# Retention and two MLPs on one core: the hand-kept order table of all 2,323 operations is replaced by another one

## The chip, the cores and the metric

One Trainium2 chip, one core of it. The metric is the device time of one execution in microseconds (us). The kernel before has a median of 588.84 us over three runs (587.54 to 589.17).

## The reference

The input is a retention layer (2 batches, 8 heads, 768 positions, head size 64), and its output x, 1,536 tokens by 512, goes through two MLPs of hidden size 2,048. The first has a rational activation, the second x times sigmoid(x).

```python
for t in range(S):
    state = gamma[None, :, None, None] * state + np.einsum('bhd,bhe->bhde', k[:, :, t], v[:, :, t])
    y[:, :, t] = scale * np.einsum('bhd,bhde->bhe', q[:, :, t], state)
...
h = x @ w_in
P = a[0] + a[1] * h + a[2] * h * h + a[3] * h * h * h
Q = 1.0 + np.abs(b[0]) * np.abs(h) + np.abs(b[1]) * h * h
x = (P / (Q + 1e-06)) @ w_out
...
h = x @ w2_in
return (h * (1.0 / (1.0 + np.exp(-h)))) @ w2_out
```

## The kernel before, in words

**Tiling.** Retention runs as 12 chunks of 128 tokens ("at0" to "at11", `attention`, L426). The MLPs work on three groups of 512 tokens. Every factor of an MLP matmul is split into a high and a low part (`xh`/`xl`, `ih`/`il`, `oh`/`ol`, `gh`/`gl`), and three products of parts stand for one product. The first MLP has 48 steps, s0 to s47 (`step`, L541), each 128 hidden units of one token group. A step is 12 matmuls into a PSUM bank h (L552; banks h0 and h1 in turn up to s19, from s20 on h0, h1, a0 and a1 in turn), a chain on ScalarE and VectorE (L564 to L574), the split of its result into `gh` (ScalarE, L583) and `gl` (GpSimd up to s48, L584), and four projections of three matmuls into the banks acc0 to acc3 (`project`, L605). The second MLP follows in the same manner, partly by sums and differences of blocks (`joint`, L705).

**The chain of a step.** The first five operations read the bank h: ScalarE takes w = |b1 h| (L564) and s1 (L565), VectorE u2 = (w + b0) h (L566), s1 times h (L568) and the next term of the polynomial (L569). Only L566 needs L564, and only L568 and L569 need L565; otherwise the order of the five is free. Then ScalarE takes u2's absolute value, the reciprocal square root and its square (L567, L570, L571), and VectorE ends with three operations (L572 to L574). Up to s16 and from s20 on these put the reciprocal into the bank h itself, so that the bank comes free for the step that is next on it (s+2, from s20 on s+4) at the end of L574.

**Weights.** Each unit u of weights, a pair of steps wide, is loaded (`weights`, L369), rounded and put together by two ScalarE passes (L397, L399) and one VectorE pass (L400, `wt<-wt,raw` in the profile), split by ScalarE (L411) and GpSimd (L416), and some units are spilled to DRAM and read back for later groups (L383, L403).

**Order.** `Flow.op` (L107) records each operation with its engine and with what it must follow by its buffers. Nothing is issued at that point. `Flow.order` (L124) decodes the table `ORDER` (L31) into a permutation of the record, asserts that each operation stands behind those it must follow, and the operations are issued in that order. Each engine runs its own instructions first in, first out, and SyncE issues all DMAs in that order. So the table sets the queue of each engine, and where two engines use one PSUM bank, who goes first. `Op.bank` marks the bank of each ScalarE or VectorE operation that uses one (L117).

```python
places = np.frombuffer(zlib.decompress(base64.b85decode("".join(ORDER))), np.uint16)
done = [self.ops[n] for n in places]
assert all(o.place < f.place for o in done for f in o.feeds)
```

Of the kernel before, what the change touches and what calls it, by code (L numbers as in the profile page):

```python
# [28 lines left out]


ORDER = (  # L31
    'c-jru^TQBk7l7e&p2IiW%eJ{{wY+TGwpOi{wq-Bdwr$%sx7@b)egDG!({;y#G>{e$VgNuahzl{nAPxkG3<B}Nfgm*`f;^BAGC*QT4-EMs0elDfAP',
# [4 lines left out]
    'hV^kMj0eG5m=zf-U;(U&!*MPo$Lcr&M#CTQJr+j7k)W6jCqr!<1u3u@j)Cl01dCz|Oo>0>PuLu%KwX>wQ(+>E#s=6Bd*Gii9g1N~?1_!AHRi;s*b',
    '7_XH0X_eF*p8>v!D+ChPki}w#DLD0>|LbI0tgzA2=50K}no}lW+#ihH*F&XF@yN3GJ~1E`$mABX-0^uo(JaKkSdAa3Yq%`Pc;O;VkTg18^p;fnRV',
    'S4#Fj{0B7SOoPv|_Ph5x_aRK~_opBS+hqbT_mf&LCf}62XSc-FTJuJhe&={BFYS@ZR!ZzHFD{v(?#csF(R^blZiH*ZbXc2Z{)6gpHfYrDg_uv}ri',
    'rsM)%)?>W1&82ZJdGo;T{w$(aXGXMdvOI!#qoFsr{Q+k2y5{IUc_^F4>!R++<>jaP<(*vaXQ||M|d7D;bq*9o8by}30H9)Gz;r+dgu_^hlkiLbPb',  # L40
    '1a4mJ;4;4wbIr+5ty<8|yF-r~%#6;9xc&@nv2=lC9X!%@6}@9+S=z**rhTpa$z5BMK$0}21&NBo3;<7b>5j^IhWiMQ|-?tw38p-uRTyC8lzh>^k_',
    ')ZpPIMh@R_FC4>&5G6znZ*Xo%5Tb>IAyJ4PmWJC1p>0?aILr$%Ld=jjBnjVz`C%U<4avf5>=a^!9-(Jg7LMbBkUV4vnL@^pB4iCIL#mKDbPoF=OU',
    'M?ohe(h*<On&#<q!geg&|J38ghj~;Y#>E<PLGeoKPeb4jA%;q9I;b9)1YLLh<lpxEZd65}{-$6)J>Ep<+lMDu;9-Zzvc};mWWo#14x>ny@<b3b(_',
    'pP&E_?)xw&PHdG1KLyb@~)C#4;A?O|YhT36m=o9jXexZN3AASyX!hrBgC=>3472&5aF#H|{g<nIy@JFZ{u7~nrT^JcggwbJe7!}5babZj-8`g)|G',
    '(J2G8^Xr0DGUh{!i}&cJP41%!LT_T4h_Qaa4g&nTf_12IFt($L%mQxYzxD}p>QNT4GAeO#i65NQaAwj!sM_$#G^E{Bb*2?LwtH3o`uBpI_wO)LIQ',
    'db64A+!gpdxxchoSv`hU2j^jp{+-h{VdPdF8r{tQ#Y=^!*TObO|T=v|l=-iHt2OgJ0<37P0X*c<)|nQ0U&89fP35%h037qU_o`a6u~|H8-cDWs*s',
    'l%29s5&9e=QDjO+mqJn67cPW9I6YO8<dlL&a1P2z59kM~Ma3uzeGSFwN6JOHX@4j|7egK@NqH$M)uuLdJ^+0SKT|&X66#VkdP;36C8eU_T!%_g1}',
    'aVYsXjHJ81$CfQ7p<xWhgoop!SrSI?`|4iDFV&Do6FGA$6edsX8^HpQtl+p~lpe`cpS*LItTQjpTkbfPSH7)SO1qXsSrRb9Wj@m8cL^q0PL72hp!',
    'ImIl)hszEhr4E;^zsRwQ2@ic+P@@!g5bEql}rE%1nc5*cu!+W?gRiK_Uj9O6(+D|R15A~wHw4Eo?Tv|YrXdMlwg*1;Q({J=U^`?<DpVreNT1?}36',
    'K$X=^e1hkUA%-2&{R4^(`Ykop@X!Pj?gmtgD%omI!fDUJMHC5w47GZc)m=B=@=cSE3|{I(LXeUM$mLxMYCun&7__5FP)%|bds*qDSFJiXdiFo|L7',  # L50
    '`JksEZAPSY9MO{-}SMQ~zXL$~NNeWBYFnIrKh`btmu8%5!09G&k_5(ZAncj+EI<sJMN$CpI%jL*?o%EC`*FYTl6I4URO7#x$6GjiY*9E)RfR!+&p',
    'sW=X&X67`Uo$u2HdPwJ~DE~!oC@w$eZ2SW!khGkWUs5iP#|b3|7vprCoAdB1dPc>$1iz!_^dpz#Qk<9baejV5uc-<P8!J0E;}^V}({pLA%GLNiJ)',
    '#2KoU3ygF3UAJJ}2NroRBkf56-{^xdqqYTHKOra~*EQ<+wGs;kNt}Kc>1|kIQpA?#YRz7Z>3|oQX5?1pb~2bAA3m-$_krAg{PR_vH@Un>+H)+<^O',
    'VBbmraq#^g?zqu1H<jTCCD{)1xz>T>nH{nLynfvo39>9O{WS+{ua6@^`wWPKrl_|W47jt77$aQ2IPv<2(gAec^e#5`=OJ2syc_vqu<g%0x@+_XsE',
    'BFW><wIOmR&rBW#of6pcjJrvmb>r}9?FAxHLu}0e2EY9F}}>lc`c`qb$o(P@+qz-)#Vyr;p_a4-}6=e!2j}pJfDZL$UIIZb9o~#;PrfiPxC)~lW*',
    '~DzQZ*nrPP;Za)y&hHK{92q`AzMC9;9f@+QtB7x*L36BU=G(o#P0XO55-Vse+~ODp-pUpbOQmIZQ;zi}E#Ez6{hv=xwZe4ZcheQqtAWTC8<w31$;',
    'NK{EDc_o8HljyQs@<|NIF9qcx2YJMQ3JMF!7}+A5C8K1Ln6gqbOCeb+1>}1vEQ@4~oR(O!SXRka$s$FhsGOClaz=iTVlq~;N;Zinv1O;kl{j)vvP',
    '*GUCpTq<Y?B9aN!Ckl$tk&{yp)n0QdWMHTXI{r%QU$o<7B*SkPC88F3S~}AopdXT$Kt^S}IBzDJMV4bSWXb<dHm->rzr?$PT$Etmoy6T$8(UNG8i',
    '9nIeZpRrH2Tlvy%cX3BH<CP!qqm_C+0a#X&`F#+8x5&A?TYbHgFr7z^E1dXCmHIhCP(rCJ0_Q@PMA@Ah49FT*OQZs87&8j&yx@OZKG=|33IGSDK>',
    'R<9+K1go;M{;RQZ72Uq9{pQV=}YM>rzD}Cl-Ke`UddbeDF4Z4$)Wi)z82Hsnn)9C7x_`+X#sVuqxm&~7Se*6MC)l?Evb36m42_OHI25`HriM}Nol',  # L60
    'RD?WMk^)$g>emeC?wR-0-Qt)k_$p%&FfT39=311+J=^e0WB$uy}Z*NmD$TWBZktfO_fw$xJEMXTyq9izYNZ(2>$Yb8ymJ+!BG)ArgyyXycQD&w@e',
    '{-Mpat4`95+D>O^Fa1Ra>SP_M6LgAB)KU7Uc95yMLr3T)-K@Q}tMt(=T0tvnd9A56w3gP^6*^xB=`8Ig)3l=;)2%vFr|YjeOnS&{?I|mDmoCtqx=',
    '?rPBHgBY^@JYR#oAxC>puNi`)PmetHX4#4%H#LOqc6fU8>h~iJsI|IzU$IFLF-jY9Hw?YqYPN*Lk`}=jeVNuP^kJKG*lUR@dtWy`ZP{fF9KAdQs2',
    'lA96_l(i=KlM#v!fTR-R#{Z0PUt9nUO+7%7<T5oDE`B?_aQN5+VOD7@gCvUX3jFeyHi9Xebx=wHFBTZ$a<c_i()`XV8p6O#9EiYB<l_s*pmewxoK',
    'YC9i%<ZivwZZaEli3jYtar7fm9ixEoh7&X+ReJ!1D$QDEsdqH()O>anWeKbmfpJCN9|#~ZI1n9ne3B((YaRMzUnvaWB=bRi)0xrvPHE@7S}RbG|O',
    'V~EV@Op_!h&mS!T;_Wi6lOus9aWs#s3TYL%^=Rki$9(283HTWAGro>jA$me;CVA**QLTYdY{8dweMX}zqb^|Ra-+iKf#D{OTvm*ufyR>TI_5-VYS',
    'ZILy%hE~g3*a~Z8Ev=I+wbeG?I$K@)!4_D5`^A2?mA1;(*dS|WgY8$VXUlA;HMW6P)SB9QyJTJLstvJWw%FEMD;sC6?VgRdHg?&5w?C|{MfDqY+a',
    '}lpTW9y}ipB7aHrzT`6WeAtZG(-lYc|71+HW?|9@!n+WRESOC-O=5(C*rGn`yHwwwLhD*3PzAdwXVMY_x5)j<&<T^O(NJp4epDZd2^3CH1|w(~j7',
    '4i{sO5ti7<Qw#)WeG(T$l?JtY&vHX~o^u)f~l6W#dZs+Z#jj~tvx1F%J_S#bTbo<jvdpW;lmHnMvu#@(WeX}?AubndRxSrgr_(hB76&(G&9k4@|(',
    '#v=xukQa@MUU^1y{gynkM_ZWNAc5k*bZ8HPvzA-fv0xzvzEp`*%?dg>^1!-&+28pl-Kffp25Yld2K&u8NIG&_UvBA>v;~(<azz8)%OP8$n$v?Z|I',  # L70
    'G^yf^VL_SxLk&6{~n&+QRj%nNuyZ|W_)xOec5-qH*CK>ywcc_q*9+x=HR?VbD&ALoPpNB`6JdMj`4t-Z5%@xq?Rb9qs3<L&$hFXCN&h<Ed$-rn1K',
# [889 lines left out]
```

## Time and profile before

| | before |
|---|---|
| median of three runs | 588.84 us |
| profiled execution | 586.15 us |
| its span, first to last instruction | 584.3 us |
| TensorE (PE) busy | 568.2 us, 97% |
| VectorE (DVE) busy | 436.2 us, 75% |
| ScalarE (ACT) busy | 405.4 us, 69% |
| GpSimd (POOL) busy | 179.9 us, 31% |

The span runs from the first to the last instruction; 1.85 us of the execution lie around it. PE is TensorE's matmuls, and the end of a matmul is modelled. In the waits, "PE h L552 <- DVE s L345" means that TensorE stood still before a matmul of L552 into h, until a VectorE instruction of L345 that wrote s had ended. L330, L338 and L345 are lines of the helpers `act`, `tt` and `stt`, through which most ScalarE and VectorE operations go; the names of their buffers tell them apart.

### The profile page before, as it was taken

The page shows a single profiled execution, that of the slowest core. Times are in us where ns is not written, and L with a number is a line of the kernel's source. Part 1 is how long each engine was busy: PE and PEld are TensorE (multiplying, and loading weights), DVE is VectorE, ACT ScalarE, POOL GpSimd, SP SyncE. Part 2 cuts the span into 40 slices and gives each one's busy share as a digit, 9 for nine tenths or more (in the row PEclk, how much of TensorE's full clock was granted, in tenths as well). Part 3 has the DMA queues.
Part 4 walks back from the last instruction along what each step waited for, and adds up shares of the span by engine and source line. Part 5 has one row for each costly group of instructions (what it writes and reads, how often), then busy time and mean ns, then how long its engine had stood idle before and what let it go on. Part 6 is the DMA issues. An engine that isn't in the chain of part 4 may idle for free.

```text
span 584.3 us, 8254 instructions
## 1 busy us (share of the span) xinstructions
PE 568.2 (97%) x2908; PEld 464.4 (79%) x2908; DVE 436.2 (75%) x679; ACT 405.4 (69%) x697; POOL 179.9 (31%) x143
## 2 busy tenths in 40 slices
...
GB/s 272 344 359 250 260 282 174 140 61 85 108 73 87 130 72 17 2 91 85 7 180 146 215 204 247 270 224 173 115 102 126 134 83 91 54 37 209 294 38 73
DMA packets 42161, 86.36 MB, mean 148 GB/s; under 512 B 4230, under 2 KB 4358, under 8 KB 42120
## 3 DMA queue, kind: packets, MB, share of 16 engines
...
q8 instruction: 23, 0.38, 0.2%
q14 instruction: 18, 0.15, 0.1%
...
## 4 chain that ended last, share of the span: by engine, by line
PE 77%; ACT 10%; DVE 9%; DMA 2%; issue 1%; SPq 0%; ACTq 0%; DVEq 0%
PE acc L605 38%; PE h L552 12%; PE a L552 9%; PE h L768 7%; PE a L768 7%; ACT h L330 2%; DVE s L345 2%; DVE u L345 2%; ACT s L330 1%; DVE wt L345 1%; DMA vn<-in_v_dram 1%; DVE s L338 1%; ACT w L330 1%; ACT raw L330 1%; DVE h L345 1%
## 5 line engine op out<-in xcount | busy, mean ns | idle before, releaser
L338 POOL TENSOR_TENSOR gl<-s,gh 128x512 fp32r<-128x512 f32 x48 | 63.7, 1330 | 117.2 <-ACT gh L330 68.3
L605 PE MATMUL acc<-gh,oh 128*128 128x512 f32 x192 | 75.7, 394 | 0.0
L605 PE MATMUL acc<-gl,oh 128*128 128x512 f32 x192 | 75.0, 391 | 0.2 <-POOL gl L338 0.2
L605 PE MATMUL acc<-gh,ol 128*128 128x512 f32 x192 | 74.8, 390 | 0.0
L605 PE MATMUL acc<-oh,gl 128*128 128x512 f32 x192 | 74.7, 389 | 0.0
L605 PE MATMUL acc<-oh,gh 128*128 128x512 f32 x192 | 74.7, 389 | 0.0
L605 PE MATMUL acc<-ol,gh 128*128 128x512 f32 x192 | 74.7, 389 | 0.0
L552 PE MATMUL h<-xh,ih 128*128 128x512 f32 x168 | 67.1, 400 | 5.5 <-DVE s L345 5.3
L552 PE MATMUL h<-xl,ih 128*128 128x512 f32 x168 | 65.6, 390 | 0.0
L552 PE MATMUL h<-xh,il 128*128 128x512 f32 x168 | 65.5, 390 | 0.0
L345 DVE SCALAR_TENSOR_TENSOR wt<-wt,raw 128x512 int32<-128x512 int32 x64 | 51.1, 809 | 18.8 <-ACT raw L330 13.1
L416 POOL TENSOR_TENSOR il<-wt,ih 128x512 fp32r<-128x512 f32 x36 | 47.7, 1331 | 38.1 <-ACT ih L411 36.1
L416 POOL TENSOR_TENSOR ol<-wt,oh 128x512 fp32r<-128x512 f32 x36 | 48.8, 1362 | 25.1 <-ACT oh L411 20.5
L330 ACT ACTIVATE raw<-raw,par 128x512 int32<-128x512 uint32 x64 | 48.4, 759 | 2.6 <-DMA raw<-in_moe_w_in_dram 2.4
L345 DVE SCALAR_TENSOR_TENSOR s<-s,par,h 128x512 f32<-128x512 f32 x65 | 48.2, 745 | 1.5
L552 PEld LDWEIGHTS h<-xh,ih 128*128 128x128 f32 x168 | 31.5, 188 | 16.2 <-DVE s L345 8.7
L330 ACT ACTIVATE wt<-raw 128x512 f32<-128x512 f32 x64 | 42.1, 661 | 3.0 <-DMA raw<-in_moe_w_out_dram 1.1
L330 ACT ACTIVATE gh<-s 128x512 fp32r<-128x512 f32 x56 | 35.1, 628 | 12.3 <-DVE s L345 5.2
L605 PEld LDWEIGHTS acc<-gl,oh 128*128 128x128 f32 x192 | 36.0, 188 | 8.5 <-POOL gl L338 1.0
L605 PEld LDWEIGHTS acc<-gh,oh 128*128 128x128 f32 x192 | 36.0, 188 | 8.1 <-DVE raw L338 0.3
L605 PEld LDWEIGHTS acc<-oh,gl 128*128 128x128 f32 x192 | 36.0, 188 | 7.6
L605 PEld LDWEIGHTS acc<-oh,gh 128*128 128x128 f32 x192 | 36.0, 188 | 7.5
...
## 6 DMA issues: line engine op xcount, KB each, us to landing
...
```

The costliest lines, as they stand in the source:

```text
L330: lambda: nc.scalar.activation(out=out_, in_=in_, func=func, **kw),
L338: op(eng, dur, rank, lambda: e.tensor_tensor(out=out_, in0=in0, in1=in1, op=alu), reads, writes, port)
L345: lambda: nc.vector.scalar_tensor_tensor(out=out_, in0=in0, scalar=scalar, in1=in1, op0=op0, op1=op1),
L416: e.tensor_tensor(out=sl.t[nm + "l"][:, us], in0=wt.t, in1=sl.t[nm + "h"][:, us].bitcast(F32), op=ALU.subtract)
L552: nc.tensor.matmul(h.t, sl.t[w][:, ws], x[g].t[:, c, :], start=(n == 0), stop=(n == 3 * KD - 1))
L605: nc.tensor.matmul(a.t, a1, a2, start=(first and n == 0), stop=(last and n == 2))
L768: nc.tensor.matmul(b_.t, w[0](c, wlo), x[0](c, xlo), start=(start and n == 0), stop=(n == 5), skip_group_check=True)
```

## The change

The table `ORDER` gets another content: the operations, their buffers, their dependencies and the code that issues them stay as they were. The search that made the new table kept the accesses of ScalarE and VectorE to each PSUM bank in program order, that is, in the order of issue. The strings can't be read by eye; decoded with the three lines above, the two tables compare so:

| queue | operations | at another place | largest move, places | first and last place that differ |
|---|---|---|---|---|
| TensorE | 541 | 154 | 12 | 4, 198 |
| ScalarE | 695 | 300 | 57 | 3, 341 |
| VectorE | 679 | 265 | 133 | 1, 314 |
| GpSimd | 139 | 55 | 13 | 7, 90 |
| SyncE (DMAs) | 268 | 99 | 16 | 0, 125 |

The last TensorE place that differs is the matmul group at 251.2 us of the profile. What the prediction speaks of, decoded:

- Start: SyncE's first loads were qT (at0), qT (at1), vn (at1), two rows of constants, kT (at0), cst; they are qT (at1), vn (at1), a row, vn (at2), cst, a row, qT (at0), kT (at0). On VectorE, the scaling of vn (at1), which needs cst, moves from place 7 to place 1, ahead of the memset of `ones` (place 2) and of `causal` (place 3).
- Ahead of s13's matmuls TensorE no longer has two projections (s9 m2, s10 m3); ahead of the end of s11's chain VectorE no longer has one masking of at11.
- Ahead of s16's matmuls one projection fewer stands (s13 m3 and s12 m0 leave, s12 m1 comes); ahead of the end of s14's chain VectorE no longer has the build of `ident` (L835), but the weight pass of unit 9's second half.
- Ahead of s18's matmuls one projection more stands (s14 m1); ahead of the end of s16's chain `ident` leaves, and a weight pass of unit 10 comes.
- Ahead of s24's matmuls one projection fewer stands; ahead of the end of s20's chain `ident`, one operation of s22 and two of s21 leave.
- Ahead of s32's matmuls nothing changes; ahead of the end of s28's chain two operations of s30 leave. Ahead of s36's matmuls nothing changes; ahead of the end of s32's chain three operations come (the sum of a part out of acc0, and one operation each of s33 and s34).
- Turns: in a step's first five operations the bank passes from ScalarE to VectorE once, or three times (ScalarE, VectorE, ScalarE, VectorE). Three times in the old table: s1, 6, 7, 9, 11, 14, 16, 17, 19, 21, 22, 24, 27, 30, 32, 34, 35. In the new one: s1, 5, 8, 12, 20, 21, 23 to 30, 32, 34, 35. In all others of s0 to s37 it passes once.

```diff
--- before.py
+++ after.py
@@ -29,49 +29,49 @@
 
 
 ORDER = (
-    'c-jru^TQBk7l7e&p2IiW%eJ{{wY+TGwpOi{wq-Bdwr$%sx7@b)egDG!({;y#G>{e$VgNuahzl{nAPxkG3<B}Nfgm*`f;^BAGC*QT4-EMs0elDfAP',
-    'HoIq>vnPLllS#xgaw{gXj<ewV(tPfMie&(m^Ij38|nA6ojl$2!4bV@I7RK!%!CTLJl|r3b7$4l!Kq32$Y1XkPWiKDX0zA;V9IE!cZFOKruK2$Dla',
...
+    'c-jru1H%yJ769Pm_k7u2w#`+m<z?HpwQ9ArEqmFvZQHiF<+jCp|Hbp9fwX`S1M&btdWZ=C@gRUhT!;*bAQt2Ufy9sjQbQ8R2(dvSJ}^XqgpdI8Lm',
+    'bErNg*oag5>ZWB!g&B0y04gC;-u+AY_JgkP=csRwx8H;76zhWuO`yhAdDO%EI?xkPWg!ZO92npd^%oqmUPVf+BDXs>3O$38kS96oz7O0*XTgr~xO',
...
 )
```

## Rows read from the trace of the kernel before

**Rows 1.** The page: busy time of TensorE.

```profile
PE 568.2 (97%) x2908; PEld 464.4 (79%) x2908; DVE 436.2 (75%) x679; ACT 405.4 (69%) x697; POOL 179.9 (31%) x143
```

**Rows 2.** Busy time by stretch: length, then busy us of each engine.

```profile
0.00:45.00 45.00, 38.72 (x431) 32.78 (x432) 33.87 (x60) 25.05 (x45) 15.34 (x17) 0.96 0.90 323
45.00:185.00 140.00, 134.54 (x741) 106.06 (x739) 116.48 (x169) 119.93 (x204) 71.50 (x55) 1.00 0.44 155
185.00:256.00 71.00, 70.57 (x310) 58.06 (x311) 58.91 (x89) 57.73 (x100) 31.10 (x24) 1.00 0.19 64
256.00:584.30 328.30, 324.40 (x1429) 267.45 (x1427) 226.91 (x363) 202.67 (x352) 62.01 (x47) 1.00 0.41 139
```

**Rows 3.** Waits of TensorE: us in total, times, longest.

```profile
PE h L552 <- DVE s L345: 5.3, 9, 1.2
```

**Rows 4.** Timeline of TensorE: the starts of s13, s16, s24 and s36.

```profile
125.17 0.50 PE L552 MATMUL h<-xh,ih 128*128 128x512 f32 x1 [0.48 <-DVE s L345]
...
143.70 0.50 PE L552 MATMUL h<-xh,ih 128*128 128x512 f32 x1 [0.39 <-DVE s L345]
...
185.41 0.50 PE L552 MATMUL h<-xh,ih 128*128 128x512 f32 x1 [0.46 <-DVE s L345]
...
251.88 0.39 PE L552 MATMUL h<-xh,ih 128*128 128x512 f32 x1
```

**Rows 5.** Busy time from just after s13's, s16's, s18's, s24's start to 256 us.

```profile
125.30:256.00 130.70, 129.03 (x574) 104.13 (x575) 108.38 (x157) 109.56 (x186) 59.74 (x45) 1.00 0.22 77
143.90:256.00 112.10, 110.82 (x481) 89.57 (x481) 92.71 (x135) 93.43 (x159) 50.30 (x38) 1.00 0.21 73
155.40:256.00 100.60, 99.87 (x436) 81.33 (x437) 82.46 (x121) 84.54 (x144) 44.76 (x34) 1.00 0.21 73
185.60:256.00 70.40, 70.38 (x310) 57.88 (x310) 58.31 (x88) 57.12 (x98) 31.10 (x24) 1.00 0.20 64
```

**Rows 6.** Chain that ended last: nine matmuls, three projections, start and us.

```profile
188.43 2.04 PE acc L605 x9
```

**Rows 7.** Groups of VectorE from 45 to 190 us: count, busy us, mean ns.

```profile
L345 DVE SCALAR_TENSOR_TENSOR wt<-wt,raw 128x512 int32<-128x512 int32 x25 | 21.1, 856 | 2.8 <-ACT wt L330 2.8
L345 DVE SCALAR_TENSOR_TENSOR u<-w,par,h 128x512 f32<-128x512 f32 x20 | 14.9, 743 | 4.8 <-ACT s L330 2.7 <-ACT w L330 1.8
L338 DVE TENSOR_TENSOR s<-s,h 128x512 f32<-128x512 f32 x20 | 13.7, 683 | 7.6 <-ACT w L330 4.4 <-ACT s L330 3.2
...
L338 DVE TENSOR_TENSOR am<-a,causal 128x512 f32<-128x512 f32 x10 | 6.7, 684 | 0.0
```

**Rows 8.** Timeline of VectorE: `ident`, and the end of s32's chain.

```profile
133.12 1.01 DVE L835 TENSOR_TENSOR ident<-causal 128x127 f32<-128x127 f32 x1
...
249.09 0.75 DVE L345 SCALAR_TENSOR_TENSOR s<-s,par,h 128x512 f32<-128x512 f32 x1
```

**Rows 9.** Waits of ScalarE from 45 to 185 us: total, times, longest.

```profile
ACT s L330 <- DVE u L345: 7.2, 5, 3.3
```

**Rows 10.** Waits of VectorE from 185 to 260 us, the longest in total.

```profile
DVE s L338 <- ACT s L330: 3.9, 4, 1.5
```

**Rows 11.** Timeline of VectorE, then of GpSimd, at 151 us.

```profile
151.47 1.59 DVE L345 SCALAR_TENSOR_TENSOR wt<-wt,raw 128x512 int32<-128x512 int32 x1
...
151.23 1.29 POOL L338 TENSOR_TENSOR gl<-s,gh 128x512 fp32r<-128x512 f32 x1 [0.93 <-POOL ol L416]
```

**Rows 12.** Instructions of L345: durations ns min/median/max, first and last start.

```profile
L345 DVE SCALAR_TENSOR_TENSOR s<-s,par,h x65: 733/747/750, 34.1 to 317.4; 128x512 f32<-128x512 f32 x65
L345 DVE SCALAR_TENSOR_TENSOR wt<-wt,raw x64: 675/686/1743, 21.7 to 408.4; 128x512 int32<-128x512 int32 x64
```

**Rows 13.** Timeline of the start: VectorE, then TensorE.

```profile
6.33 0.23 DVE L833 TENSOR_SCALAR causal<-cst 128x128 f32<-128x128 f32 x1 [4.80 <-DMA cst<-in_consts_dram]
...
7.92 0.68 DVE L338 TENSOR_TENSOR vn<-vn,cst 128x512 f32<-128x512 f32 x1
...
6.17 1.07 PE L839 MATMUL acc<-t,ones 1*64 1x512 f32 x4
```

More of the change, by code (lines that the diff above doesn't have):

```diff
@@ L31 @@
 ORDER = (
-    'c-jru^TQBk7l7e&p2IiW%eJ{{wY+TGwpOi{wq-Bdwr$%sx7@b)egDG!({;y#G>{e$VgNuahzl{nAPxkG3<B}Nfgm*`f;^BAGC*QT4-EMs0elDfAP',
-    'HoIq>vnPLllS#xgaw{gXj<ewV(tPfMie&(m^Ij38|nA6ojl$2!4bV@I7RK!%!CTLJl|r3b7$4l!Kq32$Y1XkPWiKDX0zA;V9IE!cZFOKruK2$Dla',
-    'WfC^9wib7rZ0Zv1CI02QRK3s%)a28I&d8i1N;4(CW2GAI)z!hi+7oZ8;fTm!04Q@emXaqN*61<0hpcUMPXm}hx!gX+L4Q=5*^n?g(1D~J;M8dn!6',
-    '}mtSjE*t!0X&3r&<!3zOK1<B;0bhxcF+MjLr3@kPa!V$g3_1-dqZse7ka?2@ED#!ABcic@j3hlS0N7eh0kyYeufwD7sSUeFbMvJe$XG{;Y&z>U*Q',
-    '{6#K9052LRwN@CpV(B20y4@gAhcG?*5XVmeHSZ{Zz$hv_i`CdM+D2b19tKpY17FfR^=*N_p*VGXQ|nXn*M!hpZQ?=TJuVSX%+v2ZNBfhw38CqWjh',
@@ L37 @@
[L37 to L71, printed above, removed]
@@ L72 @@
-    'fA8x9{AVBG-MyEO^xi(+d-(7En-BLfKGuhMKfma+{TJWm_r0et@|8Zpr}`A1?4x|NPxCoG*Jt@epXrl)p-=Z2KF=5X8Q<Zne77(0v%b?;`yOB6^L',
-    '>FY^X0zO&v_p|;$Qr!Z*Y!y<gfgr|Km4&qd)L{zRCCddSBz~e64Tut-i%K`+0xtm;9*z>&N^*zu=espda!Be%O!uNk8FN{FGnwoBqsi`4fNc5B;`',
-    'Z_3M7e@A+MS=`Z{*|Jz^tSC@!S{>|U`XV-`i{@&mHpZpjRBjT;cj0h2tA|gjXMAV3A5wRkoL`09U2#<(}_#gcDp%V',
+    'c-jru1H%yJ769Pm_k7u2w#`+m<z?HpwQ9ArEqmFvZQHiF<+jCp|Hbp9fwX`S1M&btdWZ=C@gRUhT!;*bAQt2Ufy9sjQbQ8R2(dvSJ}^XqgpdI8Lm',
+    'bErNg*oag5>ZWB!g&B0y04gC;-u+AY_JgkP=csRwx8H;76zhWuO`yhAdDO%EI?xkPWg!ZO92npd^%oqmUPVf+BDXs>3O$38kS96oz7O0*XTgr~xO',
@@ new lines @@
+    'TF4Tjf@B=h}i%<$q!x?A>XQ48jhf8o7>O&Q{0p;NWyobhc1)4%DXb2UdIoyJq5bz&p1ko@8k3$o1yaq9_610Zf@DZY8TZn}Bp(nJ22havSL3@aaU',
+    '7-cEgNM)yp1>oBjh&zibb}7i8LmS|_yAGxDLjTA@C=^AzwjS?hI4QiqGET5i@l)_^o7#+1>)d6cmaRG-*5+hg|F}pl3+ZHg+D`C><94?@E3RqgCP',
+    '~>!32mn2>Qb-D1%p_BBsVSK$r%TVqSa)10gb&!}^#W(_%gx0s|l&euu+gEM&m9P!Pw%P{@ddFc}Vq%2)}1!c6!Z{0@TUu>w}XaZm%R;Uvh91@JYb',
+    '!0PxtW=6(|FabtD7W@MeVOC6xhJ~>iu7~7U1dHMi*aJsGHmrriu_m^_+L#>^;$#>F&2co0f!3H3M`JJi9j8D`oCgiCFHVJq_!}0(KVdHP#8y}w*F',
+    'sJlgN<+@RK*3Lm>YB9G?)%!@egc+ZE+6t#-Fhi&Vq3`17^Z($blnq0=C2U*au7EBIt)dVt;Im9k3%##3on*7sDtVfSs@|&c_+}3l79VxBwU8BHW1',
@@ new lines @@
+    'eurqeW)vyGY;u2Vln{YGkfGxNT>tJ`B58JRQF2}979arE=T!rJY8+O5&I0+}?6kG#;;tu>3cj5+Ejg4p-G@+%i3y0xp+>MQC7OuhNFckOTU7U?8p',
+    '(&lk6>tHk;#^z>dvP9~!E@Mxrr|~GLK|Td+{g8J59i<re1zw5Gd#dnbO|rxLwt-wupO;~C)kn(;}&>|S8yw=#cp&J*I|2_j@R%RzQwN8ny%wc*nq',
+    'pC1MS28coYxe34D*wu{*uP1NZ_v(qGtyw!^>p0sq0n_#b}6>GTOdV>7ye5zv;DW{^>!oA?F4;w?Og$8Z}sMbO_klV0KxTuhNDGR3FccoJt(6pBjG',
+    'C;=s+U2q4Z(_D%{vuO`Br+Ji+zF`vjj(~d5d|E&&=@ssUIrIiI5K>}FN-;@jA0#89Sd@`6(J6e5@n|VsrcRWcQcy}_%1l{k31y{hl!~%b4$4V|Xf',
+    '=ILohcXProt4PdeSP2LqE_Ox=%%@7%ijJbd|19dP+-q=o(d^qEwvXQaV~lKhklmNc-VB<)s_6oGMWXDoLfNGF73fbdyTcTIxk*s37I1YV?$<(;})',
@@ new lines @@
+    'tedqzDq26?hYEmt#P5tN)^rd{Xg8I{KDnRS#XBt4i&_lXIvH33jPJhrqDo^F8Ed4}}Xav=vx-^J>rS&wDp3x{8Ob1{zjiG}ymNw83ItUvnA#b6E6',
+    'qh$q93DsUI1P`dM7)*i(;=Eb6DcttrsuSoCQ&_#&kbleZKES}jPB7<noKV#0dJ?{bb^xbcbt?*$tyx0N;_x@oupGlEUf&7Uej;%mR`_K%EZIyPb$',
+    'pQXczrO@8~`4rm2*SGxKTsK>yGgI!k-#Uphzo=|B2N%%5m4J*EScj-Sv)G7jt<!IAiH8ZId~3)kZ8oR#;{1<J-bI4z&2A{?2ca88cOx%e}Eq4a!-',
+    'l5+<BfirS$&ck^*8W-hnRGW+Qk6cMpaxu=wZMZGh<)8U0mEg@1lk;;)F2(IR25*r%{DA9o11`;lxF2toRQ#Ki;d=bLv}53g+=x4JV~);cxd}Jr0b',
+    'Gt_@n|W?-*X4<#G^PhkLCj0pDS`_?!wJ@AP?f7xC;Nmzj9aZ#@)F(SLMMxmj94SJVy4&UYX66c?b{XVO)d9aStxf6}UN%;qknddvZ<QCi{6EM}pS',
@@ new lines @@
+    'em*?^Vp1>`6I9KC2JdY=GD_+RI@g$zleRwiY;SIc=|KyE4Ru=JM?#-KcGylQ+qy<mqY21sq%MMw>TlfIS*QLCS5Ajys#=rALUe1@eiXP+@Jd*$6?',
+    'Yx8k=IJ~_X7EUP%ZK?gAK{~XjIZ&(e4UT;30}o3`6G|uoqUB)@;I5v&*UoK;9Y!*|KnNwnb&ZHtme~vhHvsMzRh>|E=Q7k99a^}ZjK^n`96OqdpW',
+    'A?lux{ezwlR1E-B<Mi6+tI8;=)|^NjM4V@OOn$4MlqB$KE7gkuTGW7#Ds<%#U$*m8kcQb`<1Eh1?oi)59jl1Q^lQTdDCa9nvV+2jXFplKziyyRRG',
+    'PZDYlDJJP8x8#vm{EUlB33<oQ`9~=!r6jN9ll=06Uvm{v31Z^XOkT)tNiU_Ps#KHr{D=!kbEz(6q^#7G_>w>pNkYjiJtTt^lonD$YDr6}Ep?=ol#',
+    '|xdM%v0x@|f#NJt;5kq^Bg-UQ$E~NhZlC6Xbg-EcN9Bf2TFIfxeRV(pNf2Z|NvMO9Sa6jdY?U(T37b{+3R%P%6uQsU#Jpf;5(<(nK0bXX!7KWPto',
```

21 lines of the change are left out of this document (added).

## The prediction

> **What bounds the kernel.** The page comes first: TensorE is busy for 568.2 of 584.3 us [rows 1]. The two tables hold the same matmuls, so this term can't shrink; only what TensorE stands still can. The table by stretch says where that is [rows 2]: 45.00 - 38.72 = 6.28 us up to 45 us, 140.00 - 134.54 = 5.46 up to 185, 0.43 up to 256, and 3.90 in the last 328 us. The last piece has the same TensorE order in both tables and lies mostly behind its last matmul, so it stays. The waits of TensorE name the cause of the middle piece: nine times, 5.3 us together, the first matmul of a step waited until VectorE had ended the chain of an earlier step and freed its bank [rows 3]. In the timeline such a start reads "0.48 <-DVE s L345" at s13, 0.39 at s16, 0.46 at s24 [rows 4]. So TensorE sets the pace, and nearly all that can be won lies between 45 and 256 us: 5.89 us.
>
> **What moves: the releases.** A step's start is the later of two arrivals: TensorE's, behind the matmuls queued ahead, and the release, behind VectorE's queue. I ask of each critical release how far it would let all that follows come earlier: the idle time of TensorE that comes after it in the old order (what went before it would be made good), plus the VectorE work that leaves its queue, minus the TensorE work that leaves ahead of the step, since TensorE then arrives earlier. One projection is 2.04/3 = 0.68 us [rows 6]; the VectorE operations are 0.68, 0.74 and 0.75 us [rows 7, 8]; `ident` took 1.01 [rows 8]; a weight pass is 0.69 undisturbed [rows 12]. VectorE's and ScalarE's own waits are held as they are.
> s13: 130.70 - 129.03 = 1.67 us of idle after it [rows 5], one masking of 0.68 leaves, two projections (1.36) leave: 1.0 us.
> s16: 1.28 [rows 5], `ident` against a weight pass 0.32, one projection fewer 0.68: 0.9.
> s18: 0.73 [rows 5] + 0.32 + 0.68 (one projection more ahead): 1.7.
> s24: 0.02 [rows 5] + 1.01 + 0.74 + 0.68 + 0.75 - about 1.2 (one projection fewer, and less idle inside the group): 2.0.
> s32: no wait stood before it, so its own slack is taken as 0: 0.74 + 0.68 = 1.4.
> s36: the chain of s32 ended at 249.09 + 0.75 = 249.84 [rows 8], the matmuls began at 251.88 [rows 4]: 2.04 of slack, less the three operations that come (0.74 + 0.68 + 0.68): -0.1.
> The smallest of the first five is 0.9 us.
>
> **What moves: the turns.** The new order has fewer steps before s20 in which the bank passes three times. A turn has a price: before the second ScalarE pass of such a step ScalarE waited for VectorE's u2, 7.2 us in all between 45 and 185 us [rows 9]. Eight of s6 to s19 are such steps in the old table, two in the new. 7.2/8 = 0.9 us for one; the chains of two banks run side by side on the same two engines, so an idle moment of one is partly filled by the other. The price lies between 0 and 0.9; I take the middle, 0.45. Ahead of the release of s13 and of s16 the new table has two such steps fewer (3 for 5 up to s11, 4 for 6 up to s14), of s18 three, of s24 four, of s32 one, of s36 none, since from s23 to s29 it has more. With 0.45 each: s13 1.9, s16 1.8, s18 3.1, s24 3.8, s32 1.9.
>
> **Queues that move too.** At the start VectorE scales vn (at1) before it sets `ones` and `causal`. In the old order cst arrived at 6.33 us, and TensorE's product with `ones` began at 6.17 [rows 13]. Were cst to come no earlier, `ones` would wait for 6.33 + 0.68 us, which costs 0.8 to 1.0 us. But three large loads stand ahead of cst in place of four, so it comes earlier; I take 0 and keep 1.0 for the range. The other loads move by at most 16 places past others of their own size, and GpSimd's by 13; GpSimd is busy for 71.50 of 140 us there [rows 2] and has time to make a late one good. I take 0, the cover being that idle time. `ident` goes behind 210 us, where no release takes it in that stood still.
>
> **The sum.** s16 and s32 let the rest come 1.8 to 1.9 us earlier. s36 alone forbids it, if VectorE keeps its clock time. It need not: from 185 to 256 us VectorE is idle for 71.00 - 58.91 = 12.1 us [rows 2], much of it for ScalarE, whose passes begin at ends of matmuls (3.9 us in one group of waits [rows 10]); come the matmuls earlier, these do too. I take 1.8 us off the profiled 586.15 us: 584.35 us. That execution lies 2.69 us below the median of 588.84, and with the same distance the median after is 587.0 us, 0.31% less. With the turns at 0 the gain is 0.9, at 0.9 each it is 2.3 (s32): 586.5 to 587.9. What a measurement of this kernel can tell from no change is about 0.3%, 1.8 us, so the forecast lies at that edge.
>
> **Rivals.**
> More is won: the new order lets the chains run so far ahead that most of the 5.3 us of waits for the banks [rows 3] go. Half of them is 2.7, all 5.3; priced at 4.0: 584.8. For it: two steps with three turns among s6 to s19 in place of eight. Against: the releases of s13 and s16 have little work taken from ahead of them.
> Nothing is won: s36's release holds, VectorE arriving there as late as before, because three operations were put ahead of it. 588.9. For it: it is the only release with work added and no matmuls. Against: its 2.04 us of slack and the idle time of VectorE before it.
> It gets slower: VectorE and GpSimd come into each other's way more often. A weight pass that began while GpSimd worked took 1.59 us [rows 11] where the median is 0.69; the pass that reads the bank h, s<-s,par,h, never took more than 0.75 [rows 12]. From 45 to 190 us the 25 weight passes had a mean of 0.856 [rows 7], 25 x 0.17 = 4.2 us over, about five such meetings. The new table puts a weight pass ahead of s16's and another ahead of s18's release. Each new meeting costs a release 0.9 us. With two the gain is gone, with four it is -1.8: 590.6. The point is more than two new meetings ahead of s16 or s18. Against: the moves are as likely to part old pairs.
> By the Trainium skill, SBUF — State Buffer, section "SBUF: two separate sides", VectorE with two SBUF inputs and GpSimd share a port pair as an exclusive lock, and the later one blocks for the whole instruction. By that rule the meetings are all or nothing, as 1.59 against 0.69 agrees, and every weight pass set beside a GpSimd pass is such a risk.
> That the change doesn't do what it says is hardly open: the table is what is decoded.
>
> **How the numbers follow.** Forecast 0.45, more 0.20, nothing 0.20, slower 0.15. Of the forecast's own range (586.5 to 587.9) some three fifths lie below 587.07, the bound of 0.3%. Faster: 0.27 + 0.20 = 0.47; same: 0.18 + 0.20 = 0.38; slower 0.15. The range reaches from 584.0, most of the first rival, to 590.6, where the slower case begins; it leaves out some 0.15.
>
> **What would show it.** Right: TensorE waits less for "DVE s L345" than 5.3 us, its idle time between 45 and 256 us falls to about 4 us, the idle time up to 45 us stays near 6.3, and ScalarE's 7.2 us of waits for u2 fall below 4. Wrong: a wait before s36 with VectorE's release behind it (nothing won); weight passes of mean over 0.95 us between 45 and 190 us (slower); or waits of projections for `gl` or of matmuls for loads, which neither rival has.

## The result: 1.55% less, and the profile after

The kernel after took 579.35 us in the median of four runs (577.36 to 579.94), beside 588.19 us for the kernel before (median of four): ratio 0.9845, 95% interval 0.9813 to 0.9878. The forecast was 587.0 us in a range from 584.0 to 590.6. The sign was right; the size forecast, 1.8 us, was a fifth of the 8.8 that came, and the range missed.

The profiled executions compare as 577.36 to 586.15 us, their spans as 575.3 to 584.3. The page of the kernel after, TensorE's and the other engines' busy time (answers to [rows 1]):

```profile
PE 565.4 (98%) x2908; PEld 465.6 (81%) x2908; DVE 432.6 (75%) x679; ACT 403.9 (70%) x697; POOL 179.6 (31%) x143
```

Busy time by stretch of the kernel after, with the columns of [rows 2]:

```profile
0.00:45.00 45.00, 39.01 (x430) 32.95 (x431) 32.28 (x58) 24.43 (x44) 16.63 (x18) 0.96 0.94 327
45.00:185.00 140.00, 139.94 (x779) 113.69 (x778) 119.99 (x180) 126.55 (x216) 72.08 (x57) 1.00 0.46 158
185.00:256.00 71.00, 71.00 (x314) 58.54 (x313) 61.95 (x94) 59.58 (x104) 34.05 (x27) 1.00 0.17 60
256.00:575.30 319.30, 315.48 (x1391) 260.42 (x1389) 218.35 (x350) 193.37 (x336) 56.84 (x43) 1.00 0.42 142
```

Subtract the second column from the first and the gain can be read off. Between 45 and 256 us TensorE stands still for 0.06 us, where it was 5.89 [rows 2]. Up to 45 us it is 5.99 (6.28 before), in the last stretch 3.82 (3.90). Together that is 6.2 us of idle time less. The other 2.8 us of the 9.0 by which the span is shorter are TensorE's busy time itself, 565.4 for 568.2, at the same 2,908 matmuls. In the same 140 us ScalarE now gets 6.6 us more work done and VectorE 3.5 more: the chains run ahead.

The waits of TensorE, the longest of the kernel after. The row of [rows 3], "h <- DVE s L345", is no longer among them:

```profile
PE a L468 <- POOL ol L416: 1.6, 1, 1.6
PE h L857 <- DVE u L853: 1.5, 1, 1.5
```

The waits of ScalarE from 45 to 185 us, the longest of the kernel after (answers to [rows 9]):

```profile
ACT u L330 <- DVE u L345: 5.2, 6, 1.4
ACT gh L330 <- DVE s L345: 2.3, 2, 1.6
```

The 7.2 us of "s <- DVE u" are gone; ahead of u2's absolute value ("u <- DVE u") ScalarE waits longer than before, 5.2 us for 1.5. VectorE's groups from 45 to 190 us (answers to [rows 7]):

```profile
L345 DVE SCALAR_TENSOR_TENSOR wt<-wt,raw 128x512 int32<-128x512 int32 x26 | 20.1, 782 | 0.4 <-ACT wt L330 0.3
L345 DVE SCALAR_TENSOR_TENSOR u<-w,par,h 128x512 f32<-128x512 f32 x22 | 16.3, 743 | 2.3 <-ACT s L330 2.0 <-ACT w L330 0.2
L338 DVE TENSOR_TENSOR s<-s,h 128x512 f32<-128x512 f32 x20 | 13.6, 682 | 2.2 <-ACT s L330 1.9 <-ACT w L330 0.2
...
L345 DVE SCALAR_TENSOR_TENSOR t<-u,h 128x512 f32<-128x512 f32 x18 | 12.3, 684 | 9.8 <-ACT h L330 9.8
```

Before its passes over the bank (u and s) VectorE waited for ScalarE 4.8 + 7.6 us before [rows 7] and 2.3 + 2.2 now. Part of the wait has moved further down the chain, to where one engine needs what the other has just made: before `t` (L572), which needs ScalarE's reciprocal, it is 9.8 us (4.5 before).

**One step, seen close.** In the kernel before, s10's matmuls began at 106.01 us and had waited 1.07 us for the end of s8's chain, on the same bank. ScalarE's timeline there, in the kernel before (start, us, instruction, in brackets the idle time ahead of it):

```profile
96.58 0.68 ACT L330 ACTIVATE w<-h,par 128x512 f32<-128x512 f32 x1
100.56 0.78 ACT L330 ACTIVATE s<-h,par 128x512 f32<-128x512 f32 x1 [3.30 <-DVE u L345]
101.24 0.62 ACT L330 ACTIVATE u<-u 128x512 f32<-128x512 f32 x1
```

The first two are w and s1 of s9, a three-turn step: s1 had to wait until VectorE had read the bank for s9's u2. The third is the absolute value of s8's u2. VectorE had that u2 ready at about 98.3 us, as its timeline shows, again in the kernel before (the first s and the first u are s8's, the second ones s9's):

```profile
96.20 0.69 DVE L338 TENSOR_TENSOR s<-s,h 128x512 f32<-128x512 f32 x1 [2.05 <-ACT w L330]
...
97.59 0.74 DVE L345 SCALAR_TENSOR_TENSOR u<-w,par,h 128x512 f32<-128x512 f32 x1
...
98.85 0.96 DVE L345 SCALAR_TENSOR_TENSOR wt<-wt,raw 128x512 int32<-128x512 int32 x1
99.73 0.73 DVE L345 SCALAR_TENSOR_TENSOR u<-w,par,h 128x512 f32<-128x512 f32 x1
101.38 0.69 DVE L338 TENSOR_TENSOR s<-s,h 128x512 f32<-128x512 f32 x1 [0.91 <-ACT s L330]
```

So s8's chain stood still for 3 us behind an instruction of s9, and TensorE paid for a third of it. Between the two u2 VectorE also had a weight pass of 0.96 us; in the kernel after it stands behind the end of s8's chain. The first row shows the other kind of wait: s8 takes one turn, so VectorE's s1 h, which needs s1 alone, waited 2.05 us until ScalarE had done w too. In the kernel after s9 has one turn, with both passes of ScalarE at once, and s8 has three:

```profile
94.34 0.78 ACT L330 ACTIVATE s<-h,par 128x512 f32<-128x512 f32 x1 [0.23 <-PE h L552]
95.02 0.68 ACT L330 ACTIVATE w<-h,par 128x512 f32<-128x512 f32 x1
95.59 0.63 ACT L330 ACTIVATE u<-u 128x512 f32<-128x512 f32 x1
```

From the start of s8's u2 to the start of s10's matmuls it is 8.4 us before (97.59 to 106.01) and 7.3 after (93.63 to 100.95), and in the kernel after s10's matmuls do not wait.

### The profile page after: what moved, and what is told of

Read it like the earlier page. It is cut to its first block, busy times and chain, and to the rows that moved or that the text cites. A ratio compares the mean times of both kernels' runs of the same rounds, so it can differ in the third digit from the quotient of the medians.

```text
span 575.3 us, 8261 instructions
## 1 busy us (share of the span) xinstructions
PE 565.4 (98%) x2908; PEld 465.6 (81%) x2908; DVE 432.6 (75%) x679; ACT 403.9 (70%) x697; POOL 179.6 (31%) x143
## 4 chain that ended last, share of the span: by engine, by line
PE 91%; DVE 3%; ACT 2%; DMA 2%; POOL 1%; issue 1%; SPq 0%; POOLq 0%; DVEq 0%; ACTq 0%
PE acc L605 44%; PE h L552 17%; PE a L552 10%; PE h L768 7%; PE a L768 7%; PE a L468 1%; PE a L515 1%; DMA qT<-in_qt_dram 1%; PE a L505 1%; PE h L505 1%; DVE s L345 1%; DMA cst<-in_consts_dram 1%; PE a L493 1%; DVE wt L345 0%; PE h L493 0%
## 5 line engine op out<-in xcount | busy, mean ns | idle before, releaser
L338 POOL TENSOR_TENSOR gl<-s,gh 128x512 fp32r<-128x512 f32 x48 | 63.6, 1328 | 108.9 <-ACT gh L330 75.0
L552 PE MATMUL h<-xh,ih 128*128 128x512 f32 x168 | 66.0, 393 | 0.1
L552 PE MATMUL h<-xl,ih 128*128 128x512 f32 x168 | 65.5, 390 | 0.0
L552 PE MATMUL h<-xh,il 128*128 128x512 f32 x168 | 65.4, 389 | 0.0
L345 DVE SCALAR_TENSOR_TENSOR wt<-wt,raw 128x512 int32<-128x512 int32 x64 | 48.1, 760 | 19.1 <-ACT raw L330 14.5
L416 POOL TENSOR_TENSOR ol<-wt,oh 128x512 fp32r<-128x512 f32 x36 | 47.3, 1322 | 36.2 <-ACT oh L411 31.6
L330 ACT ACTIVATE raw<-raw,par 128x512 int32<-128x512 uint32 x64 | 48.4, 760 | 3.7 <-DMA raw<-in_moe_w_out_dram 2.0
L345 DVE SCALAR_TENSOR_TENSOR s<-s,par,h 128x512 f32<-128x512 f32 x65 | 48.5, 746 | 1.6
L330 ACT ACTIVATE wt<-raw 128x512 f32<-128x512 f32 x64 | 42.2, 663 | 5.0 <-DMA raw<-in_moe_w_in_dram 2.2
L330 ACT ACTIVATE gh<-s 128x512 fp32r<-128x512 f32 x56 | 34.9, 627 | 14.6 <-DVE s L345 6.5
L605 PEld LDWEIGHTS acc<-ol,gh 128*128 128x128 f32 x192 | 36.0, 188 | 7.5
```

Source lines behind the costliest of these rows:

```text
L330: lambda: nc.scalar.activation(out=out_, in_=in_, func=func, **kw),
L338: op(eng, dur, rank, lambda: e.tensor_tensor(out=out_, in0=in0, in1=in1, op=alu), reads, writes, port)
L345: lambda: nc.vector.scalar_tensor_tensor(out=out_, in0=in0, scalar=scalar, in1=in1, op0=op0, op1=op1),
L416: e.tensor_tensor(out=sl.t[nm + "l"][:, us], in0=wt.t, in1=sl.t[nm + "h"][:, us].bitcast(F32), op=ALU.subtract)
L552: nc.tensor.matmul(h.t, sl.t[w][:, ws], x[g].t[:, c, :], start=(n == 0), stop=(n == 3 * KD - 1))
L605: nc.tensor.matmul(a.t, a1, a2, start=(first and n == 0), stop=(last and n == 2))
```

## The experiments

All these kernels hold the same operations and differ in the table alone; the diffs are of the decoded table. w, u2, s1, "s1 h" and "next" are the first five operations of a chain (L564, L566, L565, L568, L569). In these kernels L328, L336, L343 and L550 are the lines L330, L338, L345 and L552 of the kernels before and after. Ratios are of medians, beside runs of the kernel before; waits and idle times are those of the one profiled execution of each kernel.

**Which part of the table.** Three things differ: the turns in the banks, the order of each engine's queue, and how TensorE's queue stands to the others. First the turns alone:

```diff
 s9 (likewise s6, s7, s11, s14, s16, s17, s19; every engine's queue as before)
-w, u2, s1, s1 h, next
+w, s1, u2, s1 h, next
```

> The old queue of every engine, but in s6, 7, 9, 11, 14, 16, 17 and 19 both ScalarE passes of the five first operations go ahead of VectorE's in their bank (34 places of the table differ). Theory T (the turns make the gain): ScalarE's 7.2 us of waits for u2 between 45 and 185 us go, TensorE's waits for 'DVE s L345' fall from 5.3 to under 1.5 us, and the time falls by 4 to 7 us, to a ratio of 0.988 to 0.993. Theory Q (what stands in front of the chains in the queues makes it): TensorE's waits stay above 4 us and the ratio is 0.997 to 1.000. The prediction's price of 0.45 us a turn lies between: about 1.8 us, 0.997.

Measured: 585.45 us beside 587.79, ratio 0.9960 (0.9943 to 0.9977). Then the kernel after with its turns put back:

```diff
 s9 (likewise s6, s7, s11, s16, s17, s19; every engine's queue as after)
-s1, w, s1 h, u2, next
+s1, s1 h, w, u2, next
```

> The new queue of every engine, but in s6, 7, 9, 11, 16, 17 and 19 VectorE's u2 (in s11 and s19 the product) goes ahead of ScalarE's second pass in its bank, as in the old table. Theory T: most of the gain is gone, TensorE waits 3 us or more for 'DVE s L345', ratio to the kernel before 0.992 to 1.000. Theory Q: the gain stays, ratio 0.984 to 0.987, and TensorE waits under 0.5 us.

Measured: 586.47, ratio 0.9980 (0.9962 to 0.9997). The turns alone give 2.3 us, the new queues without them 1.3, both together 8.8. Neither half is worth much by itself. The exchange isn't exact: s5, s8, s12 and s20, which take three turns in the new table, keep one on the old queues and three on the new ones, and s14 keeps its one turn in the second kernel.

```diff
-TensorE, ScalarE, VectorE, GpSimd, SyncE: old queues
+TensorE: new queue; the others: old queues
```

> The old queues of ScalarE, VectorE, GpSimd and SyncE with TensorE's new order. Theory P (TensorE's own order makes the gain, since it has other work ready while a bank is held): ratio under 0.992. Theories T and Q: the releases come no earlier while TensorE reaches s10 and s13 with 1.4 to 2.1 us less work ahead, so its waits for 'DVE s L345' grow from 5.3 to 6 to 9 us; ratio 0.999 to 1.006.

```diff
-TensorE, ScalarE, VectorE, GpSimd, SyncE: new queues
+TensorE: old queue; the others: new queues
```

> The new queues of ScalarE, VectorE, GpSimd and SyncE with TensorE's old order. Theory P: the gain is lost, ratio over 0.995. Theories T and Q: the chains are as far ahead as in the new kernel, and TensorE has at most 2 us more work ahead of a step: waits under 1.5 us, ratio 0.984 to 0.990.

Measured: 617.72 (ratio 1.0495, 1.0457 to 1.0533) and 616.65 (1.0493, 1.0462 to 1.0524). Both mixtures lose 29 to 30 us, though no TensorE group moves by more than 12 places. TensorE's order has no worth of its own that could be added to that of the other queues; it must fit them.

**Where in time.** The two tables keep close to each other: at any cut at most 15 operations are ahead of it in one and behind it in the other, at the cuts used here 3 and 5. So a table can be new up to a cut and old after it.

```diff
-places = old
+places = new[:176] + [n for n in old if n not in new[:176]]
```

> The first 176 places of the new table (up to about 42 us of the trace of before), the old table after them. Theory L (each stretch gives back what TensorE lost in it, and the stretches add up): the start's idle fell by 0.3 us between the two kernels, so 587.5, ratio 0.9995, not to be told from no change. Theory J (the gain is one of the whole table, a slip early in it puts all that follows out of step): the new start lets the old rest run better or worse, 585 or below, or 590 and above.

Measured: 588.14 beside 587.77, ratio 1.0012 (0.9991 to 1.0033): the start gives nothing that can be measured. The same with a cut at 546, just ahead of s13:

```diff
-places = old
+places = new[:546] + [n for n in old if n not in new[:546]]
```

> The first 546 places of the new table (to about 118 us of before, up to s13), the old table after. Theory L: 0.3 of the start, 3.8 us of idle between 42 and 118 us, and of the 2.8 us by which TensorE's busy time fell the share that this stretch has in the idle time, 1.8: 5.9 us less, 582.0, ratio 0.990. Theory N (each step that loses its turns is worth the same, whichever stretch it is in): 4 of the 8 changed three-turn steps are in it (s6, s7, s9, s11), half the gain, 4.4 us, 583.5, ratio 0.9925. Theory J: the seam puts the old rest out of step, under 2 us less, 586 or above.

Measured: 583.16, ratio 0.9919 (0.9889 to 0.9949). The complement:

```diff
-places = old
+places = old[:546] + [n for n in new if n not in old[:546]]
```

> The complement: the first 546 places of the old table, the new one after. Theory L: 1.4 + 0.7 us of idle and 1.0 of busy time, 3.1 less, 584.8, ratio 0.9948. Theory N: the other 4 of the 8 steps (s14, s16, s17, s19), 4.4 less, 583.5. Theory J: the late arrival of the old first part costs the new rest its fit, under 1 us less or slower, 587 or above. If L holds, the two gains of this kernel and of the one with the new first part add up to the 8.8 us of the whole change; if J holds, they add up to far less.

Measured: 586.25, ratio 0.9956 (0.9932 to 0.9980). With the cut at 729, about at s20:

```diff
-places = old
+places = new[:729] + [n for n in old if n not in new[:729]]
```

> The first 729 places of the new table (to about 158 us of before, up to s20), the old one after. Theory L: only the 0.7 us of idle after 165 us and about 0.3 of busy time are still missing, 580.3, ratio 0.987. Theory N: all 8 steps are in it, 579.3, ratio 0.985. Theory J: 583 or above, since 18 of the steps after it still go by the old table.

Measured: 577.97, ratio 0.9824 (0.9797 to 0.9850). Busy time of the kernel new up to s13, then of the one new from s13 on, in the stretches 42 to 118 and 118 to 165 us (before: 72.17 of 76 and 45.56 of 47):

```profile
42.00:118.00 76.00, 75.98 (x501) 61.29 (x497) 66.49 (x105) 69.56 (x120) 42.14 (x34) 1.00 0.64 223
118.00:165.00 47.00, 45.70 (x212) 36.24 (x212) 37.88 (x53) 40.03 (x68) 21.38 (x16) 1.00 0.25 92
```

```profile
42.00:118.00 76.00, 73.00 (x479) 58.03 (x481) 63.38 (x96) 63.39 (x109) 43.24 (x34) 0.98 0.64 223
118.00:165.00 47.00, 43.88 (x211) 35.37 (x208) 36.08 (x53) 40.91 (x70) 20.36 (x16) 0.96 0.25 89
```

In the first the idle time is gone up to 118 us and remains behind. In the second it remains ahead and grows at the cut, from 1.4 to 3.1 us in the second stretch: s13, the first step of the new part, waits 1.9 us for its bank (0.5 before). From 130 to 256 us none is left. The two gains, 0.81% and 0.44%, make 1.25% of the 1.55%, which the intervals allow to be all of it. A stretch can be changed by itself, so the gain isn't one of the whole table. The new order behind s20 adds nothing that can be measured: with it 0.9845, without it 0.9824.

The lean version leaves the old start as well:

```diff
-places = old
+places = old[:176], then what new[:729] has more, then the rest of old
```

> The new table from place 176 to 729 alone (some 42 to 158 us of before), the old one ahead of it and behind. Theory L (the stretches add up; start and end of the changed part add nothing): as with the new start, 578 to 579.5, ratio 0.983 to 0.986. Rival (the new start brings the rest into step): 582 or above.

Measured: 578.70 beside 587.60, ratio 0.9842 (0.9826 to 0.9858). The whole gain lies in the stretch from s2 to s20.

**Turns or queues, stretch by stretch.** Up to s13, the new queues with three turns put back:

```diff
 s9 (likewise s6, s7, s11; places up to 546 new, old after)
-s1, w, s1 h, u2, next
+s1, s1 h, w, u2, next
```

> The kernel with the new first 546 places (583.2), each engine's order as it is there, but VectorE's and ScalarE's passes take three turns in s6, s7, s9 and s11 again; 18 places of the table differ from it. Theory B (the bank turns and the engines' order are two halves of one edit, neither is worth much without the other): most of that kernel's 4.6 us goes, 587; TensorE's idle time between 42 and 118 us, nothing there, is 2 to 3 us again, and VectorE and ScalarE wait for each other's passes over u and s for 6 us or more, where it was 2.6. Theory Q (in this stretch the engines' order does it): 583.2, idle under 0.5.

and the old queues with one turn:

```diff
 s9 (likewise s6, s7, s11; all else as before)
-w, u2, s1, s1 h, next
+w, s1, u2, s1 h, next
```

> The kernel before, each engine's order as it is there, with one turn in s6, s7, s9 and s11 (14 places differ). Theory B: half of the 2.3 us that one turn in eight steps gave, 586.5; ScalarE's waits for VectorE's u between 42 and 118 us (4.0) go, but VectorE's own waits for ScalarE's passes over u and s (6.7) stay at 6 or more, and TensorE is idle there for 1.5 to 3 us of the 3.8. Theory T (the turns do it): 583.2, idle under 0.5.

Measured: 586.50, ratio 0.9985 (0.9964 to 1.0006), and 584.55, ratio 0.9947 (0.9930 to 0.9963). The expectation for the second was 2 us too high: here fourteen places alone bring 3.1 us, two thirds of the 4.6 that both halves bring up to s13. Busy time from 42 to 118 us, then VectorE's and ScalarE's waits for each other there, of the first:

```profile
42.00:118.00 76.00, 73.55 (x480) 59.07 (x481) 63.58 (x99) 64.19 (x111) 42.56 (x34) 0.98 0.64 224
```

```profile
DVE s L336 <- ACT s L328: 2.9, 3, 1.1
DVE u L343 <- ACT w L328: 1.6, 3, 1.3
...
ACT s L328 <- DVE u L343: 4.5, 3, 1.9
...
ACT w L328 <- DVE s L336: 1.8, 2, 1.5
```

and of the second, in which ScalarE has no such wait:

```profile
42.00:118.00 76.00, 74.70 (x501) 59.49 (x502) 66.16 (x101) 67.38 (x116) 44.47 (x36) 1.00 0.66 225
```

```profile
DVE u L343 <- ACT s L328: 3.7, 2, 2.2
DVE s L336 <- ACT w L328: 3.5, 4, 1.4
```

Add up, in each kernel, what VectorE and ScalarE wait for each other's passes over one bank between 42 and 118 us (before: VectorE 6.7, ScalarE 4.0; the largest rows of each:)

```profile
DVE s L338 <- ACT w L330: 3.6, 3, 2.1
...
ACT s L330 <- DVE u L345: 4.0, 2, 3.3
```

| 42 to 118 us | ratio | in-bank waits, VectorE + ScalarE | TensorE idle |
|---|---|---|---|
| old queues, three turns (before) | 1 | 6.7 + 4.0 | 3.83 us |
| old queues, one turn | 0.9947 | 7.2 + 0 | 1.30 us |
| new queues, three turns | 0.9985 | 4.5 + 6.3 | 2.45 us |
| new queues, one turn | 0.9919 | 2.6 + 0 | 0.02 us |

Here too s5, s8 and s12 keep three turns in both kernels on the new queues and one on the old.

What the queues do for the turns shows in the decoded tables. ScalarE's two passes over a bank, w and s1, stand next to each other in its queue (distance 1) or have passes of other chains between them:

| steps s2 to s20 | one turn, distance | three turns, distance |
|---|---|---|
| before | 1 (nine steps); s8 3, s20 4 | s9, s14 1; s7, s11, s16, s17 2; s6 3; s19 4 |
| after | 1 (twelve steps); s16, s19 2; s15 3 | s8, s12 3; s20 4; s5 6 |

With three turns ScalarE's second pass waits for a pass of VectorE, and all that is queued behind it waits too; that is for nothing where the second pass could follow at once. With one turn VectorE waits for both passes, though each of its first two needs only one; that is long where they stand apart. Up to s20 the new table gives one turn to all pairs that stand together and three to most of those apart (s15, s16 and s19 stand 2 or 3 apart and have one). Put three turns on pairs that stand together (new queues, third row) and ScalarE waits, 6.3 us. Put one turn on s6, s7, s9 and s11 of the old queues, three of them 2 or 3 apart (second row), and ScalarE's 4.0 us go while VectorE's 6.7 stay, 7.2: a gain, but not the whole one.

From s13 to s20, behind the new first part, the same two halves:

```diff
 s16 (likewise s14, s17, s19; places up to 546 new, old queues after)
-w, u2, s1, s1 h, next
+w, s1, u2, s1 h, next
```

> The kernel with the new first 546 places (583.2), and behind them the old engine orders with one turn in s14, s16, s17 and s19 (20 places differ). Theory B2 (from s13 to s20 the turns are worth nothing without the new engine orders, since VectorE then waits in the bank for ScalarE where ScalarE waited for it): 583 to 584, ratio 0.991 to 0.994, TensorE's idle time from 118 to 172 us stays at 1 us or more. Theory T2 (the turns do it, as between s5 and s13): half or more of the 5 us that the new places up to s20 add, 580.5 or under, idle there under 0.5.

```diff
 s16 (likewise s17, s19; places up to 729 new, old after)
-s1, w, s1 h, u2, next
+s1, s1 h, w, u2, next
```

> The kernel with the new first 729 places (578.0), each engine's order as it is there, but three turns in s16, s17 and s19 again (23 places differ). Theory B2 (both halves are needed): back to the kernel with the new places up to s13, 582 to 584, with VectorE's and ScalarE's waits for each other over u, s and w between 118 and 172 us rising from 2.7 to 6 or more. Theory Q2 (the engines' order does it): 578 to 579, TensorE's idle time there under 0.3.

Measured: 583.11 beside 587.31, ratio 0.9929 (0.9901 to 0.9957), and 583.02, ratio 0.9932 (0.9909 to 0.9956). Neither half alone is worth anything here: without either it was 0.9919, with both 0.9824. VectorE's waits from 118 to 172 us in the kernel with one turn on the old queues:

```profile
DVE s L336 <- ACT w L328: 3.1, 2, 1.9
DVE u L343 <- ACT s L328: 2.5, 3, 0.9
```

and ScalarE's there in the kernel with three turns on the new queues:

```profile
ACT s L328 <- DVE u L343: 3.6, 2, 1.9
ACT w L328 <- DVE s L336: 1.2, 1, 1.2
```

| 118 to 172 us | ratio | in-bank waits, VectorE + ScalarE | TensorE idle |
|---|---|---|---|
| old queues, three turns | 0.9919 | 4.6 + 3.2 | 1.30 us |
| old queues, one turn | 0.9929 | 6.3 + 0 | 2.54 us |
| new queues, three turns | 0.9932 | 3.7 + 4.8 | 1.70 us |
| new queues, one turn | 0.9824 | 2.7 + 0 | 0.05 us |

Again only both together take the sum of the waits down. Among the other three rows the larger sum doesn't go with the larger idle time, so the sum doesn't measure the loss; and the 1.3 to 2.5 us of idle time are half at most of the 5 us by which the last row is ahead in the medians.

**Are fewer turns always better?** The kernel after still has steps with three turns. One turn in twelve of them:

```diff
 s29 (likewise s5, s8, s12, s20, s23 to s26, s28, s30, s35; queues as after)
-w, u2, s1, s1 h, next
+w, s1, u2, s1 h, next
```

> The kernel after, each engine's order as it is there, with one turn in twelve more steps that still take three (s5, s8, s12, s20, s23 to s26, s28 to s30, s35; 98 places differ). Theory B: a turn has no price of its own; between 45 and 256 us TensorE is idle for 0.06 us, so nothing is left to win: 579.4, ratio to before 0.985, or 1 to 2 us more where VectorE's passes now wait for ScalarE's. Theory N (each three-turn step costs its 1 us wherever it is): part of 12 us, 577 or under, faster than both kernels.

Measured: 595.42 beside 587.60, ratio 1.0132 (1.0117 to 1.0148), some 16 us slower than the kernel after. Neither theory expected a loss of this size. VectorE's longest wait from 165 to 260 us in this kernel, and TensorE's:

```profile
DVE u L343 <- ACT s L328: 16.0, 7, 3.4
```

```profile
PE a L550 <- DVE s L343: 6.1, 3, 3.0
```

In the kernel after that wait of VectorE is 2.3 us, and TensorE has none there. In these twelve steps ScalarE's two passes stand 2 to 11 places apart. In nine of them u2, which needs w alone, now waits for s1 as well; in s5, s8 and s28 it is s1 h, which needs s1 alone, that waits for w. So fewer turns aren't better in themselves: an edit that gained 3.1 us in four steps of the kernel before costs 16 in twelve of the kernel after. That the distance decides is argued from this and not shown: the twelve were changed at once, and in the kernel before the edit gained at distances of 1 to 3.

## Why the prediction was wrong

**What bounds the kernel: right.** TensorE's idle time between 45 and 256 us was what there was to win, and the cause was the one that [rows 3] name. All 5.3 us of it went. The sum built on it was 1.8 us; measured, idle time gave 6.2 us and busy time 2.8.

**"This term can't shrink": wrong by 2.8 us.** TensorE's busy time fell from 568.2 to 565.4. The matmuls are the same, but the profile counts part of each wait as busy time. In the kernel before, around the wait of s16 [rows 4]:

```profile
142.70 0.39 PE L605 MATMUL acc<-gh,ol 128*128 128x512 f32 x1
142.93 0.39 PE L605 MATMUL acc<-gl,oh 128*128 128x512 f32 x1
143.70 0.50 PE L552 MATMUL h<-xh,ih 128*128 128x512 f32 x1 [0.39 <-DVE s L345]
144.04 0.40 PE L552 MATMUL h<-xl,ih 128*128 128x512 f32 x1
144.27 0.39 PE L552 MATMUL h<-xh,il 128*128 128x512 f32 x1
```

In the stream the starts are 0.23 us apart, while the modelled end makes each matmul 0.39 long. From 142.93 to 144.04 it is 1.11 us where two places of the stream are 0.46: the wait cost 0.65 us and is shown with 0.39. The other 0.26 counts as busy, 0.15 ahead of the wait and 0.11 behind it. Worked out so from the starts around all nine waits it is 2.3 us of the 2.8 (0.18 each for the four that stand behind matmuls of the attention). What made up the other 0.5 us isn't settled.

**The releases: the step that failed first.** "VectorE's and ScalarE's own waits are held as they are." With that, what a release could win was counted from the few operations that left VectorE's queue ahead of it (0.9 to 2.0 us), and the smallest of these was taken for all. But those waits were the larger part: in the stretch up to s13 the two engines waited 10.7 us for each other in the banks before and 2.6 with the new order. Nor is an operation that leaves worth just its own length. Ahead of the end of s8's chain the new table no longer has the weight pass of 0.96 us at 98.85 us; in the old order it held up s9's u2, so ScalarE's pass of s9, and behind that s8's chain. That release, of s10, is one of the longest of the nine waits and isn't among those that the prediction works out. Nor did s36, which was thought to forbid more, hold anything up: TensorE's idle time from 185 to 256 us is nil.

**The turns: the step that failed second.** "I take the middle, 0.45," with bounds of 0 and 0.9, for every turn wherever it is. Measured per step: 0.8 us in s6 to s11 on the old queues (3.1 for four), 0.3 over eight steps (2.3), nothing in s14 to s19 on the old queues behind the new first part, and, in the kernel after, a loss of 1.3 us in the mean for each of twelve further steps that lost their turns (16 in all). So the price isn't a property of the turn; it changes its sign with the queues and steps around it. How far apart the two passes stand in ScalarE's queue, which could have been read from the tables beforehand, is the likely reason. The sum of turns and releases, each priced by itself, also left out that over the whole change each needed the other (2.3 and 1.3 us alone, 8.8 together).

**The start: right.** Taken at 0; the new start alone gave 1.0012 (0.9991 to 1.0033).

**The rivals.** "More is won" was the case that came, with its mechanism (most of the bank waits go), held at 0.20 and priced at 4.0 us; with all 5.9 us of idle time and the 2.8 us of busy time it should have been 8.7. What was held against it, that s13 and s16 have little work taken from ahead, looked at operations and not at waits. "Nothing is won" fell with s36, which did not wait. "It gets slower" asked for weight passes of over 0.95 us; their mean fell from 0.856 to 0.782 us.

**What stays open.** From the cut at s13 to the one at s20 the medians fall by 5.2 us (583.16 to 577.97), the two profiled executions by 2.2 (581.69 to 579.48), and the idle time that went there is 2.5. The time of the first's profiled execution is the lowest of its six and that of the second's the highest of its five; where the other executions lose more wasn't seen. Which single moves of VectorE's queue count wasn't tried, nor were the queues of ScalarE, VectorE, GpSimd and SyncE exchanged one by one.
